# A fixed instruction order, small first groups and a deferred 1/std in a fused retention and feed-forward kernel

## The chip, the cores and the metric

One core of one Trainium2 chip. The time is the device time of one execution in microseconds (us), as the median of several runs. The span is the time from the first to the last instruction in one profiled execution; it is about 2 us shorter than the device time.

## The reference, cut to what matters

Retention over 4 batches, 8 heads, 768 positions and a head size of 64, and then a feed-forward layer with a residual. The kernel takes and gives float32 and computes with bf16 operands.

```python
# retention, per batch and head
gamma = 1.0 - 2.0 ** (-5.0 - np.arange(H))
for t in range(S):
    state = gamma * state + outer(k[t], v[t])
    y[t] = scale * q[t] @ state            # scale = 1/8

# feed-forward on x = y with heads side by side, 512 columns
xn = (x - mean(x)) / sqrt(var(x) + 1e-6) * g_ln
out = x + maximum(xn @ w_ch1, 0) @ w_ch2   # 512 -> 2048 -> 512
```

Both kernels cut the 3072 rows into 24 tiles of 128 (6 for each batch). Within a tile the retention is a masked 128 x 128 product for each head; across tiles a decayed 64 x 64 state is carried. Names used throughout: **pa** is the product of k and q, **asb** its masked copy, **py** the result of retention, **pd** the tile's addition to the state, **pb** the decayed state, **MM1** the 512 to 2048 product, **MM2** the 2048 to 512 product.

## The kernel before

The program is in the order below. The order on the engines is near to it but not the same: in the trace single transposes stand between the matmuls of one MM1 run (at 46.57 us, for one), so the framework has moved some instructions. Per loop step the program works on one tile in each phase, shifted by fixed lags.

```python
    GT = 4                     # tiles in a group of MM1
    MM1_LAG = 6; MM2_LAG = 9
    ...
    for t in range(-2, NT + MM2_LAG):
        # loads of tile t+2 on GpSimd's queue, one quarter of w1 or w2 at the end of steps -2 to 5
        # vg = v * decay          (VectorE for the first tiles, then GpSimd)
        # MM1: a quarter of group (t - MM1_LAG) // 4
            for ko in range(KO):
                nc.tensor.matmul(pm1, lhsT=w1[:, ko, ho * P:(ho + 1) * P],
                                 rhs=xnt1[:, ko, :, :], start=(ko == 0), stop=(ko == KO - 1))
            nc.scalar.activation(out=h1[:, ho, :], in_=pm1, func=AF.Relu)
        # transposes of q and k; trs = transpose * decay of q
        # pa in two halves, each with its own multiply by a 0/1 mask (VectorE)
        # MM2 of tile t - 9: 16 matmuls, then osb = pm2 + x_all (VectorE), store
        # transposes of xn, then four evictions that multiply by g_ln
            for ko in range(KO):
                nc.scalar.mul(out=xnt_of[tg][:, ko, ti, :], in_=pxt[:, ko, :], mul=gln[:, ko:ko + 1])
        # py; x_all = py (ScalarE); pd; the state:
                ptmp = pd + pb_prev                # VectorE
                pb   = ptmp * g128m                # GpSimd
        # statistics of py (VectorE), then for every tile:
            nc.scalar.activation(out=rstd, in_=mv[:, 1:2], func=AF.Sqrt, bias=epsb, scale=1.0)
            nc.vector.reciprocal(out=rstd, in_=rstd)
            ... negms = -mean * rstd
            nc.scalar.activation(out=xn, in_=xg, func=AF.Identity, bias=negms, scale=rstd)
```

## Time and profile before

| | before |
|---|---|
| device time, median | 254.81 us (254.53 to 255.15; 255.1 in the run that the prediction quotes) |
| span of the profiled run | 253.1 us |
| first MM1 matmul | 43.78 us |
| one tile in the steady stage | 9.06 us; mean of twelve 8.93 us |
| last output addition starts | 249.02 us |

Four tiles of six take 9.06 us. The two around the end of a batch take 8.65 to 8.76 us: the first lacks pd, the second lacks the part of py that reads the state, and ScalarE's wait is not in the chain there.

The slices, the stretches of 10 us, the chain for one tile and the end are shown inside the prediction below. Two further lines of the page matter. The first is the chain that ended last, by engine (shares of the span); the second is the group of four evictions by ScalarE (count, busy time, mean ns, idle time ahead of it and what ended it).

```profile
PE 65%; ACT 14%; DMA 8%; DVE 5%; POOL 5%; issue 2%; POOLq 0%
...
L298 ACT ACTIVATE xntg<-pxt,gln 128x128 bf16<-128x128 bf16 x96 | 27.4, 368 | 55.0 <-PE pxt L296 54.9
```

Only 65% of the last chain is TensorE (PE). ScalarE (ACT) holds 14% of it although it is busy for only 53% of the span. Slices are counted from 0, here and in the prediction.

### The profile page before, as it was taken

The page shows a single profiled execution, that of the slowest core. Times are in us where ns is not written, and L with a number is a line of the kernel's source. Part 1 is how long each engine was busy: PE and PEld are TensorE (multiplying, and loading weights), DVE is VectorE, ACT ScalarE, POOL GpSimd, SP SyncE. Part 2 cuts the span into 40 slices and gives each one's busy share as a digit, 9 for nine tenths or more (in the row PEclk, how much of TensorE's full clock was granted, in tenths as well). Part 3 has the DMA queues.
Part 4 walks back from the last instruction along what each step waited for, and adds up shares of the span by engine and source line. Part 5 has one row for each costly group of instructions (what it writes and reads, how often), then busy time and mean ns, then how long its engine had stood idle before and what let it go on. Part 6 is the DMA issues. An engine that isn't in the chain of part 4 may idle for free.

```text
span 253.1 us, 4043 instructions
## 1 busy us (share of the span) xinstructions
PE 222.4 (88%) x1577; PEld 118.0 (47%) x1600; DVE 104.5 (41%) x249; ACT 133.2 (53%) x295; POOL 109.7 (43%) x121
## 2 busy tenths in 40 slices
PE   0534666999999999999999999999999999999993
PEld 0323444555555545545554554555455444444441
DVE  5454476256364353535435434543544231111121
ACT  5133456699484476558447546744754475333100
POOL 8948589789985373337357530330110100000000
PEclk9999999999999999999999999999999999999999
DMA  6999999999999976494998550410110011111012
GB/s 42 119 182 183 186 176 175 172 88 108 95 125 105 62 85 80 65 65 62 93 68 91 71 40 39 62 44 0 44 41 19 25 43 41 41 44 41 12 71 83
DMA packets 83106, 20.18 MB, mean 80 GB/s; under 512 B 75920, under 2 KB 80016, under 8 KB 83088
## 3 DMA queue, kind: packets, MB, share of 16 engines
q0 software_dynamic: 79104, 13.64, 69.4%
q1 hardware_dynamic: 3984, 6.30, 6.6%
q8 instruction: 12, 0.20, 0.3%
q14 instruction: 6, 0.05, 0.0%
HBM read 27.27 MB, written 6.29 MB: 133 GB/s over the span
## 4 chain that ended last, share of the span: by engine, by line
PE 65%; ACT 14%; DMA 8%; DVE 5%; POOL 5%; issue 2%; POOLq 0%
PE pm L275 33%; PE pm L219 21%; DMA qsb<-in_q_dram 8%; ACT xntg L298 6%; DVE stats L360 3%; ACT h1g L226 3%; PE pa L250 2%; ACT x_all L334 2%; PE pxt L296 2%; PE ptr L233 2%; PE ptr L235 2%; ACT rstd L364 1%; POOL ksb L90 1%; POOL vsb L96 1%; ACT trs L240 1%
## 5 line engine op out<-in xcount | busy, mean ns | idle before, releaser
L219 PE MATMUL pm<-xntg,w 128*128 128x512 bf16 x364 | 88.6, 382 | 3.8 <-ACT h1g L226 1.6
L275 PE MATMUL pm<-w,h1g 128*128 128x512 bf16 x381 | 86.3, 380 | 0.2
L226 ACT ACTIVATE h1g<-pm 128x512 bf16<-128x512 f32 x96 | 55.5, 592 | 18.8 <-PE pm L219 14.6
L219 PEld LDWEIGHTS <-w 128*128 128x128 bf16 x384 | 36.7, 98 | 46.7 <-issue 9.9
L275 PEld LDWEIGHTS <-h1g 128*128 128x128 bf16 x384 | 36.3, 98 | 43.3
L298 ACT ACTIVATE xntg<-pxt,gln 128x128 bf16<-128x128 bf16 x96 | 27.4, 368 | 55.0 <-PE pxt L296 54.9
L283 DVE TENSOR_TENSOR osb<-pm,x_all 128x512 f32<-128x512 f32 x24 | 16.6, 692 | 76.9 <-PE pm L275 76.9
L257 DVE TENSOR_TENSOR asb<-pa,cm 128x512 bf16<-128x512 f32 x48 | 30.9, 683 | 7.7 <-PE pa L250 7.6
L203 POOL TENSOR_TENSOR vg<-vsb,ks 128x512 bf16<-128x512 bf16 x17 | 19.7, 1158 | 28.8 <-PE pd L342 19.2
L90 POOL DMA_DIRECT2D ksb<-in_k_dram x24 | 21.7, 906 | 20.2 <-PE pd L342 19.8
L355 POOL TENSOR_TENSOR pb<-ptmp,g128m 128x512 bf16<-128x512 bf16 x16 | 18.6, 1161 | 27.1 <-DVE ptmp L354 27.0
L237 DVE TENSOR_TENSOR trs<-ptr,qsT 128x512 bf16<-128x512 bf16 x24 | 10.2, 424 | 35.5 <-PE ptr L235 35.4
L84 POOL DMA_DIRECT2D qsb<-in_q_dram x24 | 21.9, 913 | 5.3 <-PE pa L250 2.2
L96 POOL DMA_DIRECT2D vsb<-in_v_dram x24 | 21.9, 916 | 3.6 <-POOL vg L203 1.8
L233 PE MATMUL ptr<-idn,qsb 128*128 128x128 bf16 x96 | 11.0, 245 | 12.0 <-DMA qsb<-in_q_dram 12.0
L376 ACT ACTIVATE xn<-x_all,negms,rstd 128x512 bf16<-128x512 bf16 x24 | 19.5, 811 | 3.1 <-DVE negms L367 2.4
L360 DVE BATCH_NORM_STATS2 stats<-py 128x6 f32<-128x512 f32 x24 | 16.7, 697 | 8.1 <-ACT x_all L334 8.1
L334 ACT CAST x_all<-py 128x512 bf16<-128x512 f32 x24 | 14.3, 597 | 9.4 <-PE py L326 5.7
L240 ACT COPY trs<-ptr 128x512 bf16<-128x512 bf16 x24 | 14.0, 585 | 6.5 <-DVE trs L237 6.5
L233 PEld LDWEIGHTS <-qsb 128*128 128x128 bf16 x96 | 7.6, 107 | 17.3 <-DMA qsb<-in_q_dram 13.3
L296 PE MATMUL pxt<-idn,xn 128*128 128x128 bf16 x96 | 10.1, 233 | 3.8 <-ACT trs L240 3.7
L250 PE MATMUL pa<-trs 64*128 64x128 bf16 x192 | 12.0, 243 | 1.6 <-ACT trs L240 1.6
(42 smaller groups left out, 137.1 us busy)
## 6 DMA issues: line engine op xcount, KB each, us to landing
out_dram<-osb SPq DMA_DIRECT2D x24, 256.0 KB, 2.0
w<-in_moe_w_ch_dram POOLq DMA_DIRECT2D x8, 512.0 KB, 9.0
qsb<-in_q_dram POOLq DMA_DIRECT2D x24, 128.0 KB, 4.5
ksb<-in_k_dram POOLq DMA_DIRECT2D x24, 128.0 KB, 4.4
vsb<-in_v_dram POOLq DMA_DIRECT2D x24, 128.0 KB, 4.2
gln<-in_moe_g_ln_dram SPq DMA_DIRECT2D x1, 2.0 KB, 2.2
```

Source lines behind the costliest of these rows:

```text
L84: nc.gpsimd.dma_start(out=qsb, in_=qv[bl][cl])
L90: nc.gpsimd.dma_start(out=ksb, in_=kv[bl][cl])
L96: nc.gpsimd.dma_start(out=vsb, in_=vv[bl][cl])
L203: veng.tensor_tensor(out=vg, in0=vsb_of[ts_], in1=ks, op=ALU.mult)
L219: nc.tensor.matmul(pm1, lhsT=w1[:, ko, ho * P:(ho + 1) * P], rhs=xnt1[:, ko, :, :], start=(ko == 0), stop=(ko == KO - 1),)
L226: nc.scalar.activation(out=h1[:, ho, :], in_=pm1, func=AF.Relu)
L233: nc.tensor.transpose(ptr[:, pr, :], qsb[:, 2 * pr:2 * pr + 2, :], idn)
L257: nc.vector.tensor_tensor(out=asb[:, par_i], in0=pa, in1=cm4, op=ALU.mult,)
L275: nc.tensor.matmul(pm2, lhsT=h1[:, ho, q2 * P:(q2 + 1) * P], rhs=w2[:, ho, :], start=(ho == 0), stop=(ho == HO - 1),)
L298: nc.scalar.mul(out=xnt_of[tg][:, ko, ti, :], in_=pxt[:, ko, :], mul=gln[:, ko:ko + 1],)
L360: nc.vector.bn_stats(out=stats, in_=py.rearrange("p h d -> p (h d)"))
L376: nc.scalar.activation(out=xn, in_=xg, func=AF.Identity, bias=negms, scale=rstd)
```

## The change

The intent is to keep TensorE fed from earlier on and without small waits:

1. **Order.** Every instruction is a task with an engine, an assumed duration and a rank. A small list scheduler, run when the kernel is built, fixes the order on every engine from these.
2. **Loads.** Tiles 0 and 1, first quarter of w1, tiles 2 and 3, the rest of w1, tiles 4 to 7, w2.
3. **Groups** of 2, 2, 4, 4, 4, 4, 4 tiles for MM1 in place of six groups of 4.
4. **State** summed in PSUM over the tiles of a batch. The inverse decay goes into `vg`, and one multiply with a decay plane `bmc` gives the state that a tile uses.
5. **Decay in the mask**, and one mask multiply per tile in place of two.
6. **1/std at the output**: relu(r x) = r relu(x) for r > 0, so `xn` is only centred and scaled by g_ln, and 1/std is applied in the last addition. The square root is taken once per group.

```diff
-    GT = 4
+    GROUPS = [2, 2] + [4] * 5
+    plan = Plan({PE: 330, ACT: 130, DVE: 130, POOL: 130, SP: 0}, 1900, 5000)
@@ setup: five decay planes, nine memsets each
+    def c_bmc(c):
+        nc.vector.memset(bmc[:, c], 0.0)
+        for h in range(H):
+            o = D * (h % 2)
+            nc.vector.memset(bmc[o:o + D, c, h // 2, o:o + D], math.exp(lngam[h] * P * c))
+    bmcd = {c: a(DVE, 1000, -90 + c if c < 3 else 15 + 10 * c, lambda c=c: c_bmc(c)) for c in range(1, C)}
@@ the state
-                    nc.vector.tensor_tensor(out=ptmp, in0=pd, in1=pb_prev, op=ALU.add)
-                    nc.gpsimd.tensor_tensor(out=pb, in0=ptmp, in1=g128m, op=ALU.mult)
+                        ..., start=(c == 0 and i == 0), stop=(c == C - 2), skip_group_check=True)
+                nc.vector.tensor_tensor(out=take("pb", t + 1, ...), in0=held["pd", b], in1=bmc[:, c + 1], op=ALU.mult)
@@ normalisation
-            nc.scalar.activation(out=xn, in_=xg, func=AF.Identity, bias=negms, scale=rstd)
+            nc.vector.scalar_tensor_tensor(out=take("xn", t, ...), in0=held["py", t], scalar=mv[:, t, 0:1],
+                                           in1=gb, op0=ALU.subtract, op1=ALU.mult)
-            for ko in range(KO): nc.scalar.mul(out=xnt..., in_=pxt[:, ko, :], mul=gln[:, ko:ko + 1])
+            nc.scalar.copy(out=held["xnt", g][:, :, i4, :], in_=held["tp", ("x", t)])
@@ output
-            nc.vector.tensor_tensor(out=osb, in0=pm2, in1=x_all[:, g, :], op=ALU.add)
+            nc.vector.scalar_tensor_tensor(out=take("osb", t, ...), in0=held["mm", key], scalar=rstd[:, t:t + 1],
+                                           in1=x_all[:, t, :], op0=ALU.mult, op1=ALU.add)
@@ end
+    with tc.manual_schedule():
+        for t in plan.order():
+            t["emit"]()
```

## The prediction

> **What bounds the kernel now.** I read the forty slices first, then the busy time in stretches of 10 us, then the chain that ended last, then the timeline.
>
> ```profile
> PE   0534666999999999999999999999999999999993
> DMA  6999999999999976494998550410110011111012
> GB/s 42 119 182 183 186 176 175 172 88 108 95 125 105 62 85 80 65 65 62 93 68 91 71 40 39 62 44 0 44 41 19 25 43 41 41 44 41 12 71 83
> ```
>
> A slice is 6.3 us. TensorE is full only from slice 7, about 44 us; until slice 7 the transfer engines are full and move a nearly constant 172 to 186 GB/s. So there are two stages: one bound by loads, one by TensorE. The stretches put numbers on the first:
>
> ```profile
> core 0: us, PE busy (x) PEld busy (x) DVE busy (x) ACT busy (x) POOL busy (x), PEclk, DMA share, GB/s
> 0.00:10.00 10.00, 2.16 (x18) 1.17 (x18) 5.48 (x34) 4.14 (x7) 9.02 (x17) 1.00 1.08 67
> 10.00:20.00 10.00, 4.42 (x44) 3.13 (x45) 4.26 (x9) 2.75 (x4) 6.49 (x8) 1.00 1.57 170
> 20.00:30.00 10.00, 5.12 (x50) 3.36 (x49) 5.46 (x15) 4.81 (x10) 7.26 (x8) 1.00 1.84 181
> 30.00:40.00 10.00, 7.08 (x72) 5.53 (x72) 6.76 (x17) 5.69 (x15) 8.51 (x10) 1.00 1.84 178
> 40.00:50.00 10.00, 8.52 (x61) 5.00 (x63) 4.29 (x13) 6.46 (x14) 8.11 (x10) 1.00 1.83 178
> ```
>
> The last column is what to read: (67+170+181+178+178) x 10 us = 7.74 MB by 50 us. One q, k or v load is 0.131 MB, one weight load 0.524 MB; eight tiles (24 loads) and all eight weight loads are 7.34 MB. That much has passed by about 48 us. The weights are spread one by one between tiles, and the first matmul of the feed-forward layer (MM1 below, L219) stands behind six tiles of attention in the program, so it starts only at 43.8 us. In the chain, one period of the second stage:
>
> ```profile
> 119.10 0.34 PE pa L250 x8
> 119.44 3.56 PE pm L275 x16
> 123.00 0.24 PE pxt L296 x4
> 123.26 1.14 ACT xntg L298 x4
> 124.40 0.48 ACT x_all L334
> 124.91 0.71 DVE stats L360
> 125.86 0.29 ACT rstd L364
> 126.16 0.49 ACT h1g L226
> 126.69 1.02 PE pm L219 x4
> 128.16 0.34 PE pa L250 x8
> ```
>
> From pa to pa is 9.06 us, one tile. ScalarE is in the middle: it waits in program order for the statistics, and the eviction of MM1 (h1g) stands behind that wait, so MM1 gets its bank late. Last, the same four transposes early and late, and the end:
>
> ```profile
> 40.13 0.61 PE L233 MATMUL ptr<-idn,qsb 128*128 128x128 bf16 x4 [0.82 <-DMA qsb<-in_q_dram]
> ...
> 127.55 0.39 PE L233 MATMUL ptr<-idn,qsb 128*128 128x128 bf16 x4
> ...
> 235.00 13.98 PE L275 MATMUL pm<-w,h1g 128*128 128x512 bf16 x62
> 249.02 0.69 DVE L283 TENSOR_TENSOR osb<-pm,x_all 128x512 f32<-128x512 f32 x1 [2.76 <-PE pm L275]
> ```
>
> While TensorE only gets work as tiles land it is slow (0.61 against 0.39 us); and from the start of the last output addition to the end of the span (253.1 us) there are 4.1 us.
>
> **What the Trainium skill says.** "TensorE: Matmul & The Clock Gate", section "Wait — 56ns, not 53.3ns?": a warm matmul follows the one before by N / 2.4 GHz + 2.5 ns, 215.7 ns for 512 columns; cold by N / 1.2 GHz. The trace agrees: in the timeline the additions of successive tiles in the last stretch come at 238.66, 242.11 and 245.56 us, 3.45 us for 16 matmuls, 215.7 ns each; and the early transposes are slower by about the cold rate (4 x 51 ns = 0.21 us). "DMA: Bandwidth & Descriptors", section "Specifications": about 358 GB/s of HBM per core. The loads here cast f32 to bf16 and the profile counts the written half, so 178 GB/s written is 356 GB/s read: the load stage is at that limit, and changing the order of the loads cannot shorten it. "VectorE: DVE Perf Modes", section "The TRN2 errata — SBUF-src ops pay a fixed extra latency per instruction": an fp32 tensor_tensor takes (N+151)/0.96 ns, 691 ns at 512; the mask multiply L257 reads PSUM and takes 683 ns, so close to it.
>
> **The change, part by part.**
>
> Work of TensorE stays. At the warm rates: MM2 is 384 x 0.2157 = 82.8 us. MM1 is the same columns; the first two groups of two tiles need 128 matmuls of 256 columns at 0.109 us (14.0 us), the other five groups 320 x 0.2157 = 69.0 us. A tile of attention: q, k and x transposes 12 x 0.055 = 0.66, pa 0.34 (start to start in the trace), py 8 x 0.03 + 4 x 0.055 = 0.46, pd 0.22, together 1.68 us. Over 24 tiles, less 4 missing pd and 4 missing py parts (8 x 0.22), that is 38.6 us. The arithmetic floor is 166 + 39 = 205 us; the gain must come out of the other 48 us of the span.
>
> *Loads.* The new order is tiles 0 and 1, first quarter of w1, tiles 2 and 3, the other three quarters, tiles 4 to 7, then w2. Up to the last quarter of w2 that is again 7.34 MB. The first ten microseconds are bound by issue on GpSimd (0.9 us a load) in both kernels, so w2 is complete at about 49 us (48, and 1 us for the landing). Before, the last weight load was issued at 42.2 us and weight loads of w2 took 7.1 to 9.9 us to land: the same 49 us or later. What changes is what TensorE can do meanwhile. Each quarter of a weight has its own semaphore in the new program, so MM1 of group 0 starts when 1.31 MB have landed, near 15 us. The last quarter of w1 comes after 4 x 0.393 + 4 x 0.524 = 3.67 MB, near 28 us. By then the instruction order lets 48 of the 128 small MM1 matmuls pass. The other 80 (8.7 us) and the attention of tiles 4 to 7 (about 6.8 us) fill 28 to 44 us; MM2 of tile 0 then follows the quarters of w2 and waits for the fourth until 49 us.
>
> *From there*, TensorE has left: MM2 of tile 0, last quarter, 0.86; MM1 of five groups 69.0; MM2 of 23 tiles 79.4; attention of tiles 8 to 23, 16 x 1.68 less three missing pd and two missing py parts (5 x 0.22) = 25.8. Sum 175.1 us. 49.2 + 175.1 = 224.3, and 4.1 at the end is 228.4 us.
>
> *Steady stage.* The floor of a tile is 32 x 0.2157 + 1.68 = 8.58 us against 9.06 now: 0.48 us to win per tile. The new order puts 4 or 8 dense matmuls behind each small step. I checked each wait with measured durations. pa to py: mask multiply, now one instruction of 1,024 elements, estimate by the page's formula 1.22, plus about 0.4 for the end of pa, against 0.86 + 0.22 + 0.86 + 0.22 = 2.2 us of work between. py to the x transpose: stats 0.70 + 0.18, xn about 0.7, starts and ends 0.5, sum 2.1, against twelve MM2 matmuls, 2.6 us. Both hold, with 0.5 us to spare. ScalarE loses xn (0.81), three of four xnt instructions (1.14 in the chain becomes one of about 0.59) and most of rstd: its wait on statistics no longer stands before h1g, because 1/std is applied at the output. GpSimd loses the 16 decay multiplies (18.6 us) off the path. The state stays in PSUM, so pd of the next tile must wait for this tile's one state multiply (0.69 us) to read it; a whole tile period lies between, so that costs nothing. VectorE has per tile 0.43 + 1.22 + 0.88 + 0.7 + 0.69 + 0.7 = 4.6 us of 8.6, no bound. I still charge 0.2 us a tile for more frequent switches between large and small matmuls (0.1 to 0.2 us gaps around pd and pa in the trace), 16 x 0.2 = 3.2, and 1.5 us for missed slots.
>
> *Between the stages*, k and q of tile 8 stand behind w2: about 0.7 us of wait. Sum: 228.4 + 0.7 + 3.2 + 1.5 = 233.8 us span; device time is 2.0 us above the span before (255.1 against 253.1), so 235.8, say 235.5 us. The setup (new masks, decay planes) lies in the load stage and is not counted.
>
> **The rivals.** *TensorE late out of the load stage.* Its clock may stay cold on broken work; in the trace it was still cold at 40 us. Then 48 small MM1 matmuls and four tiles of attention before 28 us run at half rate, the 44 us become 48 to 52, and the end 238 to 242 us. Against it: from 28 us work is nearly gapless, and the trace shows the first large MM1 run becoming warm in some 2 us. *The load stage still ends it all:* if an early multiply for the state on GpSimd, which waits in line with the issues, starves the queue, w2 lands 2 to 4 us later and the time is 238 to 240. *A new wait in the steady stage:* two banks now serve MM1 and MM2, and MM1 must wait for MM2's addition. By my count that addition ends 1.15 us after MM2, and 1.3 us of other work stand between. If the fixed order misses one bank per tile as now (0.48 us), the steady stage gains nothing: 235.5 + 16 x 0.3 = 240 us. *Better than planned:* pa now alternates the two halves of the array; if the pairs overlap fully, 0.12 us x 16, with no switch cost, 231 us.
>
> **Range and chances.** The front gain is worked from bytes and counts, about 11 of the 19 us even if the steady stage gains nothing. Two rivals together give 243 to 245, still over 2% faster (under 250). Only a lost order at the front, or a slower clock under denser work, would keep it there. Range 230 to 242; faster 0.96, within 2% 0.03, slower 0.01.
>
> **What would show it.** Right: MM1 starts near 15 us, MM2 near 41; TensorE full from about 28 to 49 us apart from waits on w2; transfer rate again about 178 GB/s until 48 us; tile periods of 8.6 to 8.9 us; ScalarE out of the chain in the middle; 4 us at the end. Wrong: w2 landing well off 49 us, TensorE still busy with group 1 then, tile periods near 9.06 us, or a granted clock below 1.00.

## The result, and the profile after

| | before | after |
|---|---|---|
| device time, median | 254.81 us (254.53 to 255.15, 4 runs) | 235.2 us (234.95 to 235.3, 4 runs) |
| span | 253.1 us | 233.6 us |
| first MM1 matmul | 43.78 us | 23.10 us |
| first MM2 matmul of tile 0 | | 48.87 us |
| one tile in the steady stage | 9.06 us; mean of twelve 8.93 us | 8.69 us; mean of twelve 8.64 us |
| last output addition starts | 249.02 us | 229.46 us |

The ratio is 0.923 (95% interval 0.9216 to 0.9242). Here and below, a ratio is the mean time of one kernel's fast runs over that of the other's of the same rounds, so not quite the ratio of the medians that are quoted.

The slices of the page after; a slice is now 5.8 us.

```profile
PE   0355999999999999999999999999999999999992
DVE  6898739945965546546544645645644011110121
DMA  9999999999999999787310110110110111101212
GB/s 91 102 170 194 184 155 182 206 161 183 114 88 154 170 126 146 86 89 53 62 47 2 45 48 0 45 48 1 48 45 0 45 48 45 45 5 40 93 58 77
```

TensorE is full from slice 4, about 23 us, in place of 44 us. The transfer engines are full throughout the load stage as before. VectorE (DVE) is now 60 to 90% busy in the first five slices; before it was 40 to 50%.

Three of the stretches of 10 us of the prediction; the busy time of TensorE, right after the comma, is what to compare (4.42, 5.12 and 7.08 us there).

```profile
10.00:20.00 10.00, 5.97 (x64) 4.91 (x63) 8.90 (x28) 3.46 (x5) 9.23 (x11) 1.00 1.75 153
20.00:30.00 10.00, 8.51 (x96) 6.95 (x97) 7.86 (x15) 5.45 (x14) 8.91 (x11) 0.83 1.62 189
30.00:40.00 10.00, 9.46 (x119) 7.88 (x118) 6.02 (x11) 7.88 (x21) 8.66 (x11) 1.00 2.07 167
```

The chain that ended last, by engine, and then a tile of the steady stage in that chain (start us, duration us, what).

```profile
PE 84%; DVE 12%; issue 2%; ACT 1%; DVEq 0%
```

```profile
156.57 0.40 PE pa L343 x8
156.97 0.97 PE mm L452 x4
157.94 0.22 PE pd L398 x4
158.16 0.86 PE mm L452 x4
159.03 0.22 PE py L360 x4
159.25 0.23 PE py L364 x8
159.48 2.59 PE mm L474 x12
162.07 0.22 PE tp L415 x4
...
163.61 1.73 PE mm L452 x8
```

ScalarE has gone from the chain, from 14% to 1%. In the middle the chain is TensorE alone: each small step stands behind 4 to 12 large matmuls and waits for nobody. From this MM1 run to the next (172.30 us) it is 8.69 us; over twelve tiles (68.65 to 172.30 us) it is 8.64 us a tile, against 8.93 before.

**Where the 19.5 us of span came from.** This is an estimate from the prediction's own counts of work and the two traces. When MM1 starts at 43.78 us in the kernel before, TensorE has done q and k transposes of 7 tiles (7 x 0.44 us), pa of nearly 7 (55 of 56 matmuls, 2.3 us), py of 5 (5 x 0.46, less 0.22), pd of 5 (5 x 0.22) and the x transposes of 4 (4 x 0.22): 9.5 us of arithmetic. So 34.3 us were lost till then. After, at 52.54 us (MM2 of tile 0 is done) 174.2 of all 204.4 us of arithmetic are left, so 30.2 us have passed and 22.3 us are lost. That is 12.0 us won in the front. From there to the last addition, before took 205.2 us for 194.7 us of arithmetic (204.2 less 9.5), 10.5 us lost; after took 176.9 us for 174.2, 2.7 us lost. That is 7.8 us won behind the front. About 4.6 us of it is the shorter tile (0.29 us x 16); the rest lies before the first and behind the last of the steady tiles and was not traced further. The tail is 4.1 us in both. (The small groups need 0.2 us more arithmetic, so the two gains sum to a little more than the 19.5 us.)

**What is left in the front** is seen in the timelines. TensorE in the kernel after (start, duration, engine, line, operation; in brackets the idle time before and what ended it):

```profile
6.40 0.61 PE L325 MATMUL tp<-idn,qsb 128*128 128x128 bf16 x4 [0.41 <-DMA qsb<-in_q_dram]
10.26 0.61 PE L343 MATMUL pa<-trq,trk 64*128 64x128 bf16 x8 [3.25 <-DVE trq L330]
...
21.35 0.40 PE L415 MATMUL tp<-idn,xn 128*128 128x128 bf16 x4 [2.68 <-DVE xn L378]
...
23.10 1.06 PE L452 MATMUL mm<-xnt,w 128*128 128x256 bf16 x4
```

And VectorE in the same time:

```profile
6.66 1.23 DVE L218 TENSOR_TENSOR mask<-vsc,cm 128x1024 f32<-128x1024 f32 x1
7.94 0.48 DVE L223 MEMSET bmc<- 128x512 f32 x1
8.50 1.25 DVE L226 MEMSET bmc<- 64x64 f32 x8
9.78 0.42 DVE L330 TENSOR_TENSOR trq<-tp,qsc 128x512 bf16<-128x512 bf16 x1
```

The q of tile 0 is transposed by 7 us, but VectorE, in its fixed order, first ends the mask (at 7.9 us) and builds another decay plane (1.73 us: one memset of 0.48 and eight of together 1.25), and makes `trq` only at 9.78 us. The order was fixed with 1.0 us for a plane. Run by itself, the kernel's own model ends the mask at 5.25 us, sees the transposed q at 5.59 us and so puts a plane into the gap; in the trace VectorE ran late, and q was there before the mask was done. A last plane at 17.75 us delays the statistics of tile 1 likewise, and `xn` after it: that is the wait of 2.68 us.

### The profile page after: what moved, and what is told of

Read it like the earlier page. It is cut to its first block, busy times and chain, and to the rows that moved or that the text cites. A ratio compares the mean times of both kernels' runs of the same rounds, so it can differ in the third digit from the quotient of the medians.

```text
span 233.6 us, 4024 instructions
## 1 busy us (share of the span) xinstructions
PE 212.6 (91%) x1639; PEld 119.4 (51%) x1664; DVE 116.7 (50%) x239; ACT 104.6 (45%) x195; POOL 91.5 (39%) x108
## 4 chain that ended last, share of the span: by engine, by line
PE 84%; DVE 12%; issue 2%; ACT 1%; DVEq 0%
PE mm L474 35%; PE mm L452 34%; PE pa L343 3%; PE py L364 2%; PE tp L318 2%; DVE asb L348 2%; DVE bmc L226 2%; PE tp L325 2%; PE tp L415 2%; PE py L360 2%; PE pd L398 2%; DVE xn L378 2%; DVE bns L373 1%; DVE bmc L223 1%; DVE pb L407 1%
## 5 line engine op out<-in xcount | busy, mean ns | idle before, releaser
L452 PE MATMUL mm<-xnt,w 128*128 128x512 bf16 (+1 forms) x436 | 94.5, 350 | 1.3 <-ACT h L460 0.5
L474 PE MATMUL mm<-w,h 128*128 128x512 bf16 x371 | 87.6, 379 | 0.6
L460 ACT ACTIVATE h<-mm 128x512 bf16<-128x512 f32 (+1 forms) x112 | 59.9, 537 | 52.8 <-PE mm L452 48.7
L474 PEld LDWEIGHTS <-h 128*128 128x128 bf16 x384 | 36.0, 98 | 38.3
L482 DVE SCALAR_TENSOR_TENSOR osb<-mm,rstd,x_all 128x512 f32<-128x512 f32 x24 | 18.0, 751 | 70.0 <-PE mm L474 70.0
L348 DVE TENSOR_TENSOR asb<-pa,mask 128x1024 bf16<-128x1024 f32 x24 | 29.3, 1222 | 21.5 <-PE pa L343 21.5
L389 POOL TENSOR_TENSOR vg<-vsb,vsc 128x512 bf16<-128x512 bf16 x20 | 21.0, 1048 | 39.4 <-PE pd L398 29.0
L373 DVE BATCH_NORM_STATS2 bns<-py 128x6 f32<-128x512 f32 x24 | 16.7, 698 | 13.7 <-PE py L364 13.7
L378 DVE SCALAR_TENSOR_TENSOR xn<-py,mv,gb 128x512 bf16<-128x512 f32 x24 | 18.0, 751 | 0.9
L421 ACT COPY xnt<-tp 128x512 bf16<-128x512 bf16 x24 | 14.1, 586 | 5.7 <-PE tp L415 5.4
```

What stands on the lines that cost most here:

```text
L348: nc.vector.tensor_tensor(out=take("asb", t, [P, NPAIR, 2, P], BF16).rearrange("p i a t -> p a i t"), in0=held["pa", t], in1=mask.rearrang ...
L373: nc.vector.bn_stats(out=bns[:, t, :], in_=held["py", t].rearrange("p h d -> p (h d)"))
L378: nc.vector.scalar_tensor_tensor(out=take("xn", t, [P, DM], BF16), in0=held["py", t].rearrange("p h d -> p (h d)"), scalar=mv[:, t, 0:1], ...
L389: nc.gpsimd.tensor_tensor(out=take("vg", t, [P, H, D], BF16), in0=tile_of("v", t), in1=vsc[:, c, :].unsqueeze(2).to_broadcast([P, H, D]), ...
L452: nc.tensor.matmul(p[:, 0:n * P], lhsT=w1[:, ko, ho * P:(ho + 1) * P], rhs=held["xnt", g][:, ko, 0:n, :], start=(ko == 0), stop=(ko == KO ...
L460: nc.scalar.activation(out=held["h1", g][:, ho, 0:n * P], in_=held["mm", key][:, 0:n * P], func=AF.Relu)
```

## The experiments

Theory 1: the gain has two parts, TensorE's early start (small first groups and the modelled order) and the wait on the statistics that is gone from the steady stage; what is left in the front is VectorE's setup. Rivals: the gain comes from the order of the loads; it comes from the state that has left GpSimd; the start is held by TensorE's slow clock or by the loads, not by VectorE. All runs gave correct results. The kernel before ran next to each of them on the same chip, with a median of 254.5 to 254.8 us.

### Cheaper decay planes (on the kernel after)

```diff
 def c_bmc(c):
+    if c > 1:
+        nc.vector.tensor_tensor(out=bmc[:, c], in0=bmc[:, c - 1], in1=bmc[:, 1], op=ALU.mult)
+        return
     nc.vector.memset(bmc[:, c], 0.0)
```

(with 690 ns in place of 1000 in the model for these, and 1750 for the first.)

> Theory 1 (the front is held by VectorE: nine memsets for each decay plane, 1.73 us a plane, stand ahead of the first tiles; the planes for c=2 to 5 now take one multiply of about 0.69 us each): the three planes that stand ahead of tile 1 cost 3.1 us less, so the first small MM1 comes at about 20 us instead of 23.1, the transposes of tile 8 at about 51 us instead of 52.5, limited by the last quarter of w2 that lands near 49.8 us; time about 233.5 us (-0.8 to -1.8). Theory 2 (the front is bound by the loads, as the prediction had it): first MM1 may come earlier, but the time stays at 235.2 within 0.3. Theory 3 (VectorE alone holds the front, loads don't): -3 us, 232.

Measured: 233.42 us (233.02 to 234.57), ratio to before 0.917 (0.9146 to 0.9198). The first MM1 is at 20.96 us (23.10), MM2 of tile 0 starts at 46.59 (48.87) and the transposes of tile 8 at 50.27 us (52.54): all 2.1 to 2.3 us earlier, and the span is 2.3 us shorter. VectorE's setup was on the path, for at least this much. The multiplies were not all as cheap as planned; VectorE's timeline:

```profile
4.70 1.41 DVE L224 TENSOR_TENSOR bmc<-bmc 128x512 f32<-128x512 f32 x2
...
7.50 2.99 DVE L224 TENSOR_TENSOR bmc<-bmc 128x512 f32<-128x512 f32 x2
```

The first pair took 1.41 us, the second 2.99 us, while GpSimd's `vg` multiply ran (2.26 to 2.99 us in the four runs with these planes; the last section comes back to this).

### Groups of four only (on the kernel after)

```diff
-    GROUPS = [2, 2] + [4] * 5
+    GROUPS = [4] * 6
```

> All groups of four tiles, everything else as in the changed kernel. Theory 1 (small first groups let TensorE work during the loads): MM1 can only start after the x transpose of tile 3, near 31 us, so about 7 us of TensorE work (the 40 small MM1 matmuls, 4.4 us, and the gaps) have to be done later; time 239 to 242. Theory 2 (the gain is in the steady order, not in the groups): 235 to 236.

Measured: 239.85 us (239.09 to 240.72), ratio 0.941; MM1 starts at 31.33 us. The small first groups are worth 4.6 us. With them undone the change would still gain 15 us.

### The loads in the order of before (on the kernel after)

```diff
-    seq = [(x, t) for t in range(2) for x in "kqv"] + [("w1", 0)]
-    seq += [(x, t) for t in range(2, 4) for x in "kqv"] + [("w1", j) for j in range(1, 4)]
-    seq += [(x, t) for t in range(4, 8) for x in "kqv"] + [("w2", j) for j in range(4)]
+    seq = [(x, t) for t in range(2) for x in "kqv"] + [("w1", 0), ("w1", 1)]
+    for t in range(2, 8):
+        seq += [(x, t) for x in "kqv"] + [("w1", t) if t < 4 else ("w2", t - 4)]
```

(and the first ranks on GpSimd to match.)

> The changed kernel with the order of loads of the kernel before (weight loads one by one between the tiles from tile 1 on). Theory 1 (order of loads among the first eight tiles is nearly neutral, the kernel before already spread its weights): 235 to 237.5, as tiles 2 and 3 land 2.6 to 5 us later and w1 is complete about as early. Theory 2 (the place of the weights is a main part of the gain): over 239.

Measured: 235.43 us (235.06 to 235.76), ratio 0.924. No difference from the change: the order of the loads, named first in its description, gains nothing by itself. The weights were spread among the first tiles before, too.

### The state on GpSimd again (on the kernel after)

```diff
-  pd summed in PSUM over a batch; pb = pd * bmc[:, c + 1]            # VectorE
+  pd fresh for each tile; ptmp = pd + pb (VectorE); pb = ptmp * bmcb (GpSimd)
```

> The changed kernel with the state as before: a fresh product per tile, addition on VectorE, decay multiply on GpSimd. Theory 1 (the state sum in PSUM is off the path): 235 to 236.5 in the steady stage; in the front the GpSimd multiplies stand among the loads and may cost up to 2 us, against which four decay planes (6.9 us of VectorE) are not made. Theory 2 (the sum in PSUM carries part of the gain): over 238.

Measured: 237.57 us (237.2 to 238.48), ratio 0.933: 2.4 us slower than the change. The timelines of GpSimd and TensorE in this run say where:

```profile
45.36 0.81 POOL L272 DMA_DIRECT2D w<-in_moe_w_ch_dram  x1
...
54.56 1.89 PE L486 MATMUL mm<-w,h 128*128 128x512 bf16 x8 [0.95 <-DMA w<-in_moe_w_ch_dram]
57.07 1.02 PE L486 MATMUL mm<-w,h 128*128 128x512 bf16 x4 [0.62 <-DMA w<-in_moe_w_ch_dram]
```

GpSimd issues all loads of q, k, v and the weights. Four of the multiplies (1.15 us each) stand ahead of the last weight load, and two of them first wait for VectorE, 0.60 and 0.71 us: 5.9 us in all. That load is issued at 45.36 us, in the kernel after at 39.57 us. MM2 of the first tiles then waits for w2 four times, 2.5 us in all (0.28 and 0.65 us before the two waits shown), which is what the run lost; in the change it doesn't wait. GpSimd waits for VectorE longer later on (7.65, 7.17 and 7.54 us, all after 140 us), but a full tile there takes 8.70 us as in the change. The slices agree: the transfer rate falls to 76 GB/s in slice 6 (182 in the change), and the transfer engines stay full until slice 19 in place of 15. So the state in PSUM gains in the front, by freeing the queue of loads. The run also leaves out four of the five decay planes, so the queue alone may cost more than 2.4 us.

### An order made without durations (on the kernel after)

```diff
+        ns = ns if eng in (PE, POOL) else 1
-    plan = Plan({PE: 330, ACT: 130, DVE: 130, POOL: 130, SP: 0}, 1900, 5000)
+    plan = Plan({PE: 0, ACT: 0, DVE: 0, POOL: 130, SP: 0}, 1900, 5000)
```

The instructions are the same; only the model that orders them takes ScalarE's and VectorE's work for nearly free, and their results and TensorE's as seen at once.

> The changed kernel with the order planned as if ScalarE and VectorE took no time: attention of a tile comes in one block in the front, and in the steady stage 8 instead of 12 MM2 matmuls stand between py and the x transpose. Theory 1 (spacing by dense matmuls hides the chain from one step to the next): 8 x 0.2157 = 1.73 us against the 2.1 us that statistics and xn need, 0.4 us of wait a tile, period near 9.05, +6 us in the steady stage and some us in the front: 241 to 247. Theory 2 (1/std at the output alone removed the wait): 235 to 237.

Measured: 280.57 us (280.05 to 281.75), ratio 1.101: slower than the kernel before. In the steady stage the statistics stand in the chain as expected (start, duration, what), but they cost less: 8.71 and 8.94 us a tile here (117.50 to 126.21 to 135.15), 8.86 over twelve tiles, where I expected 9.05:

```profile
123.78 0.25 PE py L365 x8
...
124.05 0.71 DVE bns L374
...
125.00 0.76 DVE xn L379
...
125.81 0.40 PE tp L416 x4
126.21 1.73 PE mm L475 x8
```

But I expected 241 to 247 us, and the front lost far more than that allows: MM2 starts only at 86.44 us, and TensorE works in blocks with waits between them. So with the same instructions, another order costs 45 us. The run also has a lower mean granted clock (0.939); its clock row is low in several slices from 5 to 14, where TensorE has idle stretches, and full from slice 15 on. How much of the 45 us is the clock was not separated.

### 1/std at the output, alone (on the kernel before)

```diff
-            nc.scalar.activation(out=xn, in_=xg, func=AF.Identity, bias=negms, scale=rstd)
+            nc.vector.tensor_scalar(out=xn, in0=xg, scalar1=mv[:, 0:1], scalar2=None, op0=ALU.subtract)
-            nc.vector.tensor_tensor(out=osb, in0=pm2, in1=x_all[:, g, :], op=ALU.add)
+            nc.vector.scalar_tensor_tensor(out=osb, in0=pm2, scalar=rstd_all[:, g:g + 1],
+                                           in1=x_all[:, g, :], op0=ALU.mult, op1=ALU.add)
```

> The kernel before with one part of the change alone: 1/std applied at the output addition, xn made on VectorE, so ScalarE's wait for the statistics no longer stands ahead of xn (the square root stays per tile on ScalarE). Theory 1 (the steady stage lost 0.4 us a tile because h1g stood behind ScalarE's wait for statistics; the square root still waits, but the 0.81 us xn and one round trip are gone): tile period 9.06 falls to 8.8 or so, 16 tiles, time 250 to 252. Theory 2 (the order of TensorE's work is what costs): 254 to 255.5, period stays.

Measured: 254.96 us (254.37 to 255.66), ratio 1.001: nothing, where theory 1 had 250 to 252. The chain shows why; the square root is still one per tile, and ScalarE still waits for the statistics ahead of the eviction of MM1:

```profile
124.06 1.14 ACT xntg L301 x4
...
125.71 0.71 DVE stats L363
...
126.66 0.29 ACT rstd_all L367
126.95 0.49 ACT h1g L227
```

It is the same wait as before, with one instruction less behind it. Work taken off an engine gains nothing as long as the wait in its queue remains.

### 1/std at the output, with the square root once per group (on the kernel before)

```diff
+            if ty % GT == GT - 1:
+                s = slice(ty - GT + 1, ty + 1)
+                nc.scalar.activation(out=rstd_all[:, s], in_=mv_all[:, s, 1], func=AF.Sqrt, bias=epsb, scale=1.0)
+                nc.vector.reciprocal(out=rstd_all[:, s], in_=rstd_all[:, s])
+            nc.vector.tensor_scalar(out=xn, in0=py..., scalar1=mv_all[:, ty, 0:1], scalar2=None, op0=ALU.subtract)
```

> The kernel before with 1/std at the output and the square root taken once for a group of four tiles, as the change does; order of TensorE untouched. In the first try of this the square root still stood in ScalarE's queue in each tile and the period stayed 9.06 us. Theory 1 (ScalarE's wait for each tile's statistics is what the steady stage loses): in three of four tiles nothing waits, period 8.65 to 8.75 there, about 0.35 us x 14 to 16 tiles less: 249 to 251. Theory 2 (the order of TensorE's work is what costs): 254 to 255.

Measured: 252.64 us (250.79 to 253.16), ratio 0.990 (0.9841 to 0.9954). The chain now lacks the wait in three tiles of four and has it in the fourth; starts of MM2 (the one before these is at 101.08 us), and ScalarE's part in the tile with the square root:

```profile
109.85 3.56 PE pm L277 x16
...
118.55 3.56 PE pm L277 x16
...
127.25 3.56 PE pm L277 x16
...
133.68 0.30 ACT rstd_all L368
133.97 0.49 ACT h1g L228
...
136.32 3.56 PE pm L277 x16
```

The differences are 8.77, 8.70 and 8.70 us, and then 9.07 us in the tile with the square root. This is the clean test of the steady stage: where ScalarE doesn't wait for statistics, a full tile takes 8.70 us, and where it does, 9.07. The change has 8.69 us in a full tile, so inside these tiles nothing is left for its order of TensorE's work to explain. The total gain here is 2.1 us, less than the 249 to 251 us that I expected, since one tile in four still waits and the two of six around the end of a batch had no wait to lose: over twelve tiles a tile takes 8.77 us, 8.93 before and 8.64 in the change. What the change wins before and behind these tiles this run doesn't win.

### Groups of two throughout (on the kernel before)

```diff
-    GT = 4
+    GT = 2
-    MM1_LAG = 6; MM2_LAG = 9
+    MM1_LAG = 4; MM2_LAG = 8
```

(with more buffers for xnt and h1.)

> The kernel before with groups of two tiles throughout, MM1 two tiles earlier in the program, and no other change. Theory 1 (MM1 during the loads is the front gain, and it needs only an earlier place in the program): MM1 starts near 33 us instead of 43.8; in that stretch a tile comes every 5 us and TensorE has 1.7 + 3.45 us for it, so some 6 to 7 us are gained: 248 to 250. Theory 2 (small groups cost as much in matmuls of 256 columns as they gain): 253 or more.

Measured: 265.15 us (264.57 to 266.33), ratio 1.041. MM1 does start earlier, at 33.2 us in place of 43.8, but a tile then takes about 9.9 us (one run of MM2 begins at 73.87, the next at 83.77; 9.74 over ten tiles). There are 192 evictions of half the size in place of 96, and ScalarE is busy for 140.8 us in place of 133.2. In this order, groups of two lose more in every tile than they gain once; what it is in them that costs the time no run separates. That agrees with the change's choice of 2, 2 and then 4.

### What holds the front once the planes are cheap

The last three runs start from the version with cheap planes (233.42 us). They ask whether TensorE's slow clock, VectorE's remaining setup, or the loads hold what is left.

```diff
 # e5_warm: 96 matmuls of 128 columns on a zero tile, result never read, placed in TensorE's gaps
+    for f in range(48):
+        ... nc.tensor.matmul(held["mm", "fill"][:, 0:P], lhsT=wz, rhs=wz, start=True, stop=True)   # twice
 # e6_planes_late: ranks of the planes from the second on
-    -90 + c if c < 3 else 15 + 10 * c
+    -90 + c if c < 2 else 5 * c
 # e8_warm_late: both
```

> The version with cheap decay planes plus 96 small matmuls on a zero tile, never read, put into the gaps of TensorE from about 1 us until the first tiles are through. Theory that TensorE's slow clock holds the front back: with the filler the transposes and pa of tiles 0 to 3 take about 0.39 instead of 0.61 us, the first matmul of the feed-forward layer starts 1 to 1.5 us earlier than the 20.96 us measured without filler, and the time falls by about 1 us, to 232 to 232.7 us. Theory that the front is held by VectorE and by the issue of loads: the transposes may be warm, but the first of those matmuls stays at 20.5 to 21.5 us and the time at 233 to 234 us; the fillers may even delay it.

> As the version with cheap decay planes, but with the multiplies for planes 2 and later standing after the first tiles instead of before them. Theory that VectorE's setup holds the front back: in the 7.5 to 10.4 us stretch the 3 us of multiplies that collide with GpSimd are gone from ahead of tile 0's mask multiply, which starts at about 8.4 instead of 10.4 us; the first matmul of the feed-forward layer then starts at 19 to 20 us, and the time is 231.5 to 232.7 us. Rival that the arrival of tiles 2 and 3 behind the first quarter of w1, and the last quarter of w2, decide from here on: first matmul at 20.5 to 21, time 233 to 234 us.

> Both of the last two together. If both hold the front back, 231 to 232 us, with the first matmul of the feed-forward layer at about 18 to 19 us, and TensorE then waits for the last quarter of w2 at 46 to 48 us, seen as a gap in MM2 of tile 0. If neither does, 233 to 234 us.

Measured: with filler 234.17 us (233.92 to 235.22), with the other ranks 233.29 (233.19 to 233.37), with both 234.16 (233.93 to 236.09). None is faster than the version with cheap planes beyond the scatter.

The second run missed its aim: VectorE was idle at that time in the model, so the scheduler put the multiplies in the same place in spite of the ranks (`bmc` still from 4.70 and 7.50 us). It says nothing on its own question.

The first run did what it was to do. With the filler the transposes are fast from 9.4 us on, and still the first MM1 stands at 21.15 us:

```profile
9.44 0.40 PE L326 MATMUL tp<-idn,ksb 128*128 128x128 bf16 x4
...
16.84 0.40 PE L326 MATMUL tp<-idn,ksb 128*128 128x128 bf16 x4 [0.91 <-DMA ksb<-in_k_dram]
...
19.12 0.40 PE L326 MATMUL tp<-idn,ksb 128*128 128x128 bf16 x4 [0.46 <-DMA ksb<-in_k_dram]
...
20.48 0.38 PE L333 MATMUL tp<-idn,qsb 128*128 128x128 bf16 x4 [0.74 <-ACT xnt L429]
...
21.15 1.04 PE L470 MATMUL mm<-xnt,w 128*128 128x256 bf16 x8
```

So a fast array alone does not bring MM1 forward. TensorE waits for k of tiles 2 and 3, and the fixed order has MM1 behind their transposes. A reserve remains: in both filler runs k of tile 2 came later (its transposes are at 16.84 and 17.74 us, against 15.77 and 15.67 in the two runs without filler), for a cause that isn't known, and that may hide a gain of about a microsecond.

The chain of the version with cheap planes, before any filler, has the loads in it too. It runs on VectorE, through the attention of tiles 0 and 1, until 17.70 us, then by way of TensorE to the issues of GpSimd and to one load of k, for which TensorE waits until 34.30 us:

```profile
26.25 8.01 DMA ksb<-in_k_dram
```

Nor could a faster front gain much more with this load order. In the version with cheap planes, TensorE and the load queue meet (timeline of TensorE, then of GpSimd):

```profile
46.59 1.89 PE L480 MATMUL mm<-w,h 128*128 128x512 bf16 x8
...
48.54 1.89 PE L480 MATMUL mm<-w,h 128*128 128x512 bf16 x8
50.27 0.39 PE L324 MATMUL tp<-idn,ksb 128*128 128x128 bf16 x4
```

```profile
39.64 0.80 POOL L276 DMA_DIRECT2D w<-in_moe_w_ch_dram  x1
...
48.93 0.87 POOL L268 DMA_DIRECT2D qsb<-in_q_dram  x1 [1.64 <-DMA w<-in_moe_w_ch_dram]
```

The last quarter of w2 is issued at 39.64 us, and the eighth issue after it waits until 48.93 us for a weight load: read as its landing. TensorE uses that quarter in the last four of the eight matmuls that start at 48.54, so from about 49.4 us. Half a microsecond is left, which fits that none of the three runs gained. I read that reserve off two timelines; no run here shortens the load stage to show it.

**What the runs add up to.** Taken back one at a time, the small groups are worth 4.6 us, the state in PSUM 2.4 us and the order of the loads nothing that shows; put in alone, one square root per group is worth 2.1 us. That is about half of the 19.6 us of device time. The rest was not isolated: no run has the new instructions in the order that the framework gives them, so what the modelled order gains over that one is argued and not shown. The order without durations only shows that a worse one costs 45 us.

## Why the prediction was right, and where it was not

The total was right, 235.5 us against 235.2, and so was the direction of each large part. Two of its terms were wrong in opposite directions and nearly cancelled: TensorE came 1.7 us late out of the front, and 2.0 us less than charged were lost behind it. That the total is so close is luck. One of its own signs of being wrong came true all the same, a granted clock below 1.00 (0.993 on average, 0.83 from 20 to 30 us), and a second nearly did: TensorE was busy with group 1 until 48.87 us.

- **The load stage is the same in both: right.** In the kernel after GpSimd's queue shows a weight load of w2 landing at 49.88 us, against "about 49 us".
- **"MM1 of group 0 starts when 1.31 MB have landed, near 15 us": wrong.** It starts at 23.10 us. The step that failed is "The setup (new masks, decay planes) lies in the load stage and is not counted". It lies in the load stage, but VectorE is on the path there: making it cheaper took 2.1 us off the first MM1, 2.3 us off the span and, by the ratios (0.923 to 0.917), 1.5 us off the time. The rest of the 8 us was a wrong picture: MM1 doesn't start on bytes. Even with cheap planes, VectorE's work for tiles 0 and 1 lasts until 17.70 us, where `xn` of tile 1 is done. After that MM1 stands in the fixed order behind transposes of tiles 2 and 3, and even with a warm array TensorE waits for k of these tiles until 16.84 and 19.12 us.
- **"TensorE full from about 28 to 49 us apart from waits on w2": half right.** It was nearly full from 23 us on, with no such waits. It came late to MM2 (48.87 us, near 41 predicted), as the first rival said, though that one had the cold clock for the cause. The prediction had it wait for the last weights then; in fact TensorE itself was late, behind VectorE's setup: tile 8's transposes are at 52.54 us, against 49.2 + 0.86 + 0.7 = 50.8 predicted, 1.7 us late.
- **"0.2 us a tile for more frequent switches", 3.2 us, and "1.5 us for missed slots": too much.** From 52.54 to 229.46 us are 176.9 us; the prediction's work for it is 174.2 us (175.1 less the last quarter of MM2 of tile 0). So 2.7 us in place of 4.7 were lost. A full tile took 8.69 us, against a floor of 8.58 and the 8.88 that the prediction charged (8.58 + 0.2 + 0.1). "9.06 now: 0.48 us to win per tile" was read off one tile; the mean before was 8.93, and 0.29 us a tile were won.
- **"its wait on statistics no longer stands before h1g": right.** ScalarE went from 14% of the chain to 1%. The experiments sharpen it: it is the square root per tile that mattered, not the application of 1/std; moving only the latter gained nothing, and with one root per group the full tiles without it took 8.70 us against 9.07.
- **"GpSimd loses the 16 decay multiplies (18.6 us) off the path": wrong for the front.** Put back, they cost 2.4 us, because they stand in line with the issue of loads. The prediction named this only as a rival for an early multiply in the new kernel.
- **The tail, 4.1 us: right** (229.46 to 233.6).
- **The reading "178 GB/s written is 356 GB/s read: the load stage is at that limit": wrong.** In stretches of 2 us of the kernel after (us, GpSimd's busy time, granted clock, share of the transfer engines, GB/s; the share sums the times of all packets over 16 engines, so it can pass 1):

```profile
30.00:32.00 2.00, 2.00 (x3) 1.00 2.42 154
40.00:42.00 2.00, 2.00 (x3) 1.00 1.24 207
```

While weights are loaded it is 207 GB/s, with the transfer engines' share at 1.24; while q, k and v are loaded it is 154 GB/s at a share of 2.42, twice as much engine time. The figure of 178 is a mix of the two. The conclusion that loads can't be shortened by their order held (the run with the old load order, 235.43 us), for another reason: both orders carry the same mix.

## What to carry to other kernels

Setup in the load stage is free only on an engine that the first tiles don't need: write down which engine's queue the first useful matmul waits behind before calling it hidden. In the steady stage look for the wait in an engine's queue, not for its load; removing work behind a wait (1/std alone) gained nothing, and removing three waits of four gained in just those tiles. A modelled order is worth as much as its durations: with wrong ones the same instructions took 45 us more, and with cheaper planes and their durations corrected some 1.5 us less, which together with its variant with other ranks (233.3 us) is the fastest version here (233.4 us; 0.917 of before).

## What the Trainium skill lacked or had wrong

- "DMA: Bandwidth & Descriptors", section "Specifications", gives about 358 GB/s of HBM per core, as half of what a stack gives to two cores. With one core at work, weight loads that cast f32 to bf16 moved 204 to 208 GB/s as written over stretches of 2 us, about 412 GB/s as read. So the figure is no bound for a core alone; the row doesn't say so, only a remark further on in the page does. The same section's limit for short transfers (line rate from 512 B on) agrees in direction: q, k and v, in runs of 256 B read and 128 B written, moved 154 GB/s at a transfer-engine share of 2.42 against 1.24. That row gives no rate for such runs.
- "TensorE: Matmul & The Clock Gate", Part 1, says that some 3.4 us of sustained work release the clock, in a window that runs freely. The two filler runs agree: after 3.3 us of dense filler the first transposes took 0.40 us at 5.25 us in one run; in the other, after 3.6 us of it and a gap of 0.72 us, they still took 0.61 to 0.63 us until some 9 us. Gaps of 0.9 us left the array fast. After one of 2.52 us (four transposes at 17.74 us) it was at 0.61 us again, sooner than the idle window of about 3.4 us that the page gives. No page that I read says how the profile's clock column relates to this: in the kernel after that column read 1.00 from 10 to 20 us while transposes took 0.61 us, and 0.56 and 0.59 at 22 to 26 us for matmuls just as slow.
- No page that I read gives the fixed cost of a small memset on VectorE: eight of 64 x 64 f32 took 1.25 us, one every 0.16 us, and the 128 x 512 f32 one ahead of them 0.48 us.
- "SBUF — State Buffer", section "Who interferes with whom", says that a VectorE instruction with two SBUF inputs contends with a GpSimd instruction that reads SBUF. The run with cheap planes agrees, as far as its timelines show it: two f32 multiplies of 512 columns with both inputs in SBUF took 2.99 us beside a GpSimd multiply of 1.07 us, and 1.41 us earlier on, where GpSimd's own mask instruction beside them took 0.67 us in place of 0.31 us. The page has no figure for such a pair.
